# Loading q and k of the first five token pairs in other runs, with the heads paired anew

## The chip, the cores and the metric

The kernel runs on one core of a Trainium2 chip. The metric is the device time of one execution in microseconds; the time of a kernel is the median of several runs. The core's engines work side by side, each through its own list of instructions in order: TensorE (PE: matrix products; PEld is its loading of weights), VectorE (DVE), ScalarE (ACT), GpSimd (POOL), and SyncE (SP), which here mostly issues DMAs. They wait for each other through semaphores.

## The reference

Four sequences of 768 tokens, eight heads of 64. Three heads (0, 2, 6) attend causally to everything; the other five only to the first 4 tokens and to the last 64. The attention output, 3072 tokens by 512, goes through a gated feed-forward block with 1536 hidden columns.

```python
causal = rel >= 0
stream_keep = causal & (is_sink | ((rel >= 0) & (rel < window)))     # n_sink 4, window 64
mask = np.where(is_retrieval[head], causal, stream_keep)             # heads 0, 2, 6
a = softmax(np.where(mask, q @ k.T / 8, -1e9))
x = (a @ v)                      # (4, 8, 768, 64) -> (3072, 512)
g = x @ w_gate                   # (3072, 1536)
out = (g * sigmoid(g) * (x @ w_val)) @ w_out                         # (3072, 512), float32
```

All inputs are float32 in memory. The kernel computes in float16 with float32 sums.

## The kernel before, in words

The tokens are cut into 24 tiles of 128. Two tiles of one sequence make a pair; there are 12 pairs, in the order QP: (0, 0), (1, 0), (0, 1), (0, 2), (1, 1), (1, 2), and then sequences 2 and 3. A pair is what is loaded at a time: 256 tokens of q, of k or of v over all heads, 512 KB (`load`, L332; v is called x there). The weights come in 18 further loads of 512 KB. All loads are issued on SP, into a ring of 14 raw buffers; a load waits until the cast that reads its buffer's former content is done.

Each q or k load of the first five pairs (`XPE = 5`, L328) is two DMAs. One fills partitions 0 to 63 from heads 0 to 3, the other partitions 64 to 127 from heads 4 to 7; a partition gets four tokens of each of four heads, in runs of 1 KB (L338 to L344). From pair 5 on a load is one DMA over 128 partitions, in 512-byte runs of two tokens of each of eight heads (L345); v is always loaded so.

The loaded block is cast to float16 (`cast`, L402) so that a block of 128 columns holds two heads side by side. For the first five pairs TensorE transposes these blocks into PSUM (`transposes`, L442, product at L448), and ACT or DVE copies them into qT and kT, sorting the tokens out on the way (`evac`, L450). Later pairs are transposed by DMA (`dmat`, L435). The 128 rows of qT and kT are thus two heads of 64 rows. A score product (`scores`, L518, product at L533) uses 64 of the 128 rows, and the products of a unit alternate between the two halves. `PAIRS` (L165) says which heads share a block.

A tile's scores come in units of up to eight blocks of 128 by 128 (`plan`, L475). ACT takes the exponential of a unit at once (`exps`, L536). For the first four tiles (`LEAD = 4`) the mask is added into the scores by TensorE as products with an identity (`marks`, L495); later, DVE or POOL multiplies the exponentials with a mask of zeros and ones (`mask`, L547), which `FILLS` (L287) builds. The products with v (`values`, L557, product at L563) and a normalisation on DVE (`norm`, L566) follow, and the tile is transposed for the feed-forward products (`gate`, L721, product at L725; then ACT's tanh, two DVE steps, and `outproj`, product at L760). The keys and values of the 4 first tokens are copied into the first rows of later tiles (`sinks_k`, L462; `sinks_v`, L469).

Before all this TensorE runs ten products of the identity with itself, whose result is not used (`warm`, L309).

The order of the work is written out: every step is a task, and the string ORDER lists all tasks in one sequence from which each engine takes its own (L835). WAYS gives the engine of each task, SLOTS the buffer. A number of `FILL` (3700) or more in ORDER stands for a group of warming products; the kernel before has none.

Of the kernel before, what the change touches and what calls it, by code (L numbers as in the profile page):

```python
# [16 lines left out]
    "070004011K1L061I1J09031T1Q1R1S1o1p1w1x1U1V1y1W1X1f1g0A1q1r1z021d1k1e0C2K202223212B2C2Q2R2S292G2A"  # L17
    "081O1N1P1M1h1Y1Z1a1i1j0D2L2T0B1t1s1u2425261b1c1v2D2E2F2U2W2V2X2Z2a27282c2d1m1n2I2J052Y2b2h2l2m2n"
    "2r2s2o2w0h138r8s8t9192938w8x8y0n14948z90958p8u0E2O2P2N2M8m8n8o8q8v1l0g0z8c8d8e8h8i8j0y8S8T8U8X8Y"
    "0m118k8f8g8Z8l108a8V8W8b2p2q0i169697989B9C9D2e2f2i2g0G31393A3B0l1F9a9b9c9f9g2t2u2v2x0F30360o179E"  # L20
    "9F9h37383F3G3I3J0r1G9d9i9e9j3C3P3D3E3K3L0k1C9V9Q9W9X9R9S3b3c3T3H999A3U3V0J3j3r3s3t0H3234333M3N35"
    "3O3W3X3Y3Z3a0q1D9Y9Z0I3i3o9T9U3p3q3u3x3v3w3y3z0j199G9H9I9L9M9N2j3R3S2k2y2z3Q3d3e3f0p1A9O9J9P0Q55"
    "54523g3h45484E4F0x4041A9AAABAdAeAfA7ATAUACADAV0PAgAh494A2H530u0t15AOAP0w1E18AQARASAnAoAp0MA4A551"
    "580s9KA6A812AJAKAL0v1B0O1HAMAN0K3m3k3l3n0L4MAEAWAXAH0RAFAGAI0S5U590V669k9l9m9n4SAYAZAaAi4T0N4Q4R"
    "4P4N4U4V50579oAsAtAu56AvAw0Z5b4B4J4C4D42434644470cAjAk9p9q9r9s9t4G4H4K4I4LAlAmAxAyAz4Z4a4b4W4X4Y"
    "4e4f9u9v9w9x4j4p4q4u4v4c4d5T5a5Z0U4r9zA0A1A2A34m4s4O4g4t4h4n4i4k4l4oAqArAbAc0T5X5W5H5I5J5A5B5C5K"
    "B2B0B10d7o6E9y4w4x6o6l7E6n4y4z5L7G5M656C6BB3B4B5B7B8B9BABBBCBDBEBFBGBt5Q5d5j5k5e5f5g5h5iBvBwBx5Y"
    "C3BqBrBsBu0Y0bCACBCCBgBhBiBMBN0W686967ByBzBOC0C15N5O5R5P5cCDCEC2C40a7C6DBPBQBlBmBnC5C6C7BWBX5V5D"
    "5E5F5G5SBjBkBYBUBZBa6k6s6r5o5u5r5v5s5wBoBp0XC8C95l5m5p5n5q626L6M5x7I5yBbBcBdBeBf5t5z60636164BRBS"
    "BTBV7D7L7KCFCGCH7HBHBIBJBKBLCICJ6I6J6K6F6G6H6S6N6OCoCpCqCKCLCMCN0fDXDYDZCjCkClD8D9DaDbDADBDC6j6p"  # L30
    "6q7374756t6u70797JDNDODPDG0e7p7wCyCz6P71726Q6R6U6TCrCsD0D1D26Y6Z6a6d6eDQDRDDDEDFDH6v6V6W6X7SD6D3"
    "D4D5D7CeCfCgCPCQCRCSCT6m767T777A787B6w6x7r6yChCiCtCuCv6b6c7u7v7P7Q7R7MCOCwCxCmCnDSDTDU6A6f6g6h6i"
    "7N7OCUCVCWCXCZCaCYCbCc7F7U7V7WDVDW7X7g7h7a7b7c7t7d7e7f6zE4ELEJEMEOE1E2EGENEPEfEgE3E5EiEhEHEIEKEk"
    "ElEmDIDJDKEBECDLDMEDB6EpEqEjErCdDcDdDeDfDh7Y7i7j7m7kEnEo7l84857y7z81828B8380DiDjDkDmDnDo86877x8E"
    "8H8I8FDrDsDtDu7q7Z7n8K8M888N898A8C8D8LEd8GEVEWEXEQEREEEFESEYEZEsEt7s8O8J8P8QDwDxDyDzE6E7E8E9EAEa"
    "EbEcEeETEU8RFJFKFsFEFLFtFWG2FuFTFUFFDvDpFiDqDlE0FVFXFjFkFHFlFnFoFqDgFmFpFrEuFGFIFMFNGAG3G4G7G8G9"
    "GBFYFZFaFxFyFbFcFzG0G1FRG5G6FOFPFvFwFQFSFgEvEwExEyEzF0FdFeFfFhGCF1F2F4F5F6F9FAFBFCF3FDF7F8GDGEGF"
    "GGGHGIGJGKGLGMGNGOGRGPGSGTGQGWGUGVGXGY"
# [15 lines left out]
    "010523746A20796974080CAB6C17BD2493518B8DA51C93B8452163D10106040102241611232063220254440040006220"  # L54
    "616201436425612211161624043604454120646214300622320400616445611440622523226261404460004562163226"
    "112612440602263216203446045226106560612261304342246160122543246012162406140236445612242206143605"
    "0023111440102212311231000040220111550227010245020E1113A11049001182013501026303102104125F1004B212"
# [61 lines left out]
def kernel(  # L119
# [45 lines left out]
    PAIRS = [(0, 2), (4, 6), (1, 3), (5, 7)]  # L165
# [141 lines left out]
    warm_ps = []  # L307

    def warm(n=10):  # L309

        if not warm_ps:
            warm_ps.append(buf("o", [128, 512], FP, "warm"))
        for _ in range(n):
            nc.tensor.matmul(warm_ps[0], ident, ident.unsqueeze(1).to_broadcast([128, 4, 128]),
                             start=True, stop=True)
# [126 lines left out]
    def transposes(n, kd):  # L442

        tr = trs[n, kd] = buf("gv", [128, 8, 128], FH, "tr")
        for x in range(8):
            r, j = x // 4, x % 4
            to = x if kd == "q" else 4 * r + 2 * (j % 2) + j // 2
            nc.tensor.transpose(tr[:, to], hqs[n, kd][:, r, j], ident)  # L448
# [12 lines left out]

    def sinks_k(b, m):  # L462
# [3 lines left out]
        for cs, k, r in ((slice(0, 128), slice(0, 2), 1), (slice(0, 64), slice(1, 2), 0)):  # L466
# [28 lines left out]
    def marks(t, u):  # L495
# [339 lines left out]
    for number in P.order():  # L835
# [40 lines left out]
```

## Time and profile before

| | |
|---|---|
| median of three runs | 265.27 us (261.69 to 265.81) |
| the profiled execution | 262.36 us |
| its span, first to last instruction | 260.5 us |
| busy: TensorE, DVE, ACT, POOL | 243.2, 165.9, 139.2, 84.1 us |
| moved by DMA | 40.69 MB, 156 GB/s over the span |
| DMA packets | 68007 |
| q or k load of 256 KB, issue to landing (20 DMAs) | median 9.0 us (k), 8.6 us (q) |

The rows of the profile cut the span into 40 slices of 6.5 us; a digit is the busy share in tenths. A row of a timeline gives start, duration, engine, line, operation, the tiles written and read with their sizes, how many instructions are merged in the row, and in brackets the idle time before it and what ended it. A row of the windows gives the stretch and its length, the busy time and the number of instructions of PE, PEld, DVE, ACT and POOL, the granted TensorE clock, the mean share of time that the 16 DMA engines were busy (packets overlap, so it can pass 1), and GB/s. The 1.9 us between the span and the execution's time lie around the first and the last instruction.

### The profile page before, as it was taken

How to read it: one execution, taken by the hardware profiler on the slowest of the kernel's cores; microseconds unless marked ns; L12 is line 12 of the kernel's file. 1: busy time of each engine (PE TensorE's matmuls, PEld its weight loads, DVE VectorE, ACT ScalarE, POOL GpSimd, SP SyncE). 2: the span in 40 equal slices, each digit the busy share in tenths (PEclk: the TensorE clock that was granted, in tenths of full speed). 3: DMA queues.
4: the chain of work that ended last, by engine and by line, in shares of the span. 5: the costliest groups of instructions: out<-in, count | busy, mean ns of one | idle time of the engine just before them, and what ended most of it. 6: DMA issues, size and time to landing. Idle time of an engine off the chain costs nothing.

```text
span 260.5 us, 5165 instructions
## 1 busy us (share of the span) xinstructions
PE 243.2 (93%) x1998; PEld 127.9 (49%) x1998; DVE 165.9 (64%) x294; ACT 139.2 (53%) x219; POOL 84.1 (32%) x114
## 2 busy tenths in 40 slices
PE   6597987969999899989999999999999999999995
PEld 2365764446444445534464454555454554444443
DVE  2338897768497974609989678646773477883211
ACT  1568874738677476647585476644526713421120
POOL 7057945675432354183051018240014200000000
PEclk9999999979999999999999999999999999999999
DMA  6999999999699989999258841344010021101133
GB/s 152 230 236 325 285 219 264 226 273 332 155 327 276 236 168 220 300 254 255 45 77 177 193 102 20 83 116 128 1 23 20 20 64 52 69 3 40 40 126 115
DMA packets 68007, 40.69 MB, mean 156 GB/s; under 512 B 25360, under 2 KB 63504, under 8 KB 67984
## 3 DMA queue, kind: packets, MB, share of 16 engines
q1 hardware_dynamic: 66832, 38.35, 63.5%
q10 hardware_dynamic: 1152, 2.03, 2.1%
q8 instruction: 15, 0.25, 0.4%
q14 instruction: 8, 0.07, 0.1%
HBM read 28.31 MB, written 6.29 MB: 133 GB/s over the span
## 4 chain that ended last, share of the span: by engine, by line
PE 73%; DMA 13%; DVE 6%; SPq 3%; issue 2%; POOL 1%; ACT 1%; DVEq 0%; ACTq 0%
PE banks L725 40%; PE banks L760 22%; DMA raw<-in_v_dram 8%; PE banks L533 5%; PE banks L563 5%; SPq L340 3%; DMA kT<-hq 2%; DMA raw<-in_q_dram 2%; DVE e L553 2%; DVE sil L735 1%; DVE h L742 1%; POOL vt L206 1%; DVE xb L571 1%; PE banks L587 0%; POOL hq L206 0%
## 5 line engine op out<-in xcount | busy, mean ns | idle before, releaser
L545 ACT ACTIVATE e<-banks 128x1024 f16<-128x1024 f32 (+2 forms) x68 | 58.4, 908 | 31.0 <-PE banks L533 22.4
L725 PE MATMUL banks<-xt,wv_sb 128*128 128x512 f16 (+1 forms) x304 | 71.2, 371 | 2.8 <-POOL wv_sb L206 1.5
L725 PE MATMUL banks<-xt,wg_sb 128*128 128x512 f16 (+1 forms) x304 | 69.3, 368 | 1.6 <-POOL wg_sb L206 1.5
L731 ACT ACTIVATE sig<-banks 128x512 f32<-128x512 f32 (+1 forms) x76 | 43.1, 575 | 43.7 <-PE banks L725 38.5
L760 PE MATMUL banks<-wo_sb,h 128*128 128x512 f16 (+2 forms) x300 | 64.8, 371 | 0.0
L735 DVE SCALAR_TENSOR_TENSOR sil<-sig,banks 128x512 f32<-128x512 f32 (+1 forms) x76 | 49.3, 657 | 19.3 <-ACT sig L731 17.4
L742 DVE SCALAR_TENSOR_TENSOR h<-sil,banks 128x512 f16<-128x512 f32 (+1 forms) x76 | 49.0, 656 | 7.8 <-PE banks L725 5.0
L725 PEld LDWEIGHTS <-wg_sb 128*128 128x128 f16 x304 | 28.8, 97 | 33.1 <-POOL wg_sb L206 1.8
L725 PEld LDWEIGHTS <-wv_sb 128*128 128x128 f16 x304 | 28.3, 98 | 32.5 <-issue 2.8
L760 PEld LDWEIGHTS <-h 128*128 128x128 f16 x300 | 28.3, 98 | 32.4 <-issue 0.3
L553 POOL TENSOR_TENSOR e<-e,m 128x1024 f16<-128x1024 f16 (+1 forms) x12 | 22.6, 1883 | 32.4 <-ACT e L545 26.1
L553 DVE TENSOR_TENSOR e<-e,m 128x640 f16<-128x640 f16 (+1 forms) x26 | 20.3, 786 | 16.8 <-ACT e L545 16.6
L206 DVE COPY o_sb<-banks 128x512 f32<-128x512 f32 (+1 forms) x13 | 8.6, 660 | 25.0 <-PE banks L760 23.0
L206 POOL CAST vt<-raw 64x512 f16<-64x512 f32 x27 | 18.2, 675 | 17.7 <-DMA raw<-in_v_dram 14.3
L206 POOL CAST hq<-raw 128x1024 f16<-128x1024 f32 (+1 forms) x16 | 15.8, 989 | 24.7 <-DMA raw<-in_q_dram 11.9
L563 PE MATMUL banks<-vt,e 128*128 128x65 f16 x472 | 18.6, 195 | 4.0 <-POOL vt L206 3.1
L533 PE MATMUL banks<-qT,kT 64*128 64x128 f16 x472 | 21.0, 223 | 0.6 <-ACT e L545 0.4
L563 PEld LDWEIGHTS <-e 128*128 128x128 f16 x472 | 17.4, 98 | 8.4 <-issue 4.6
L204 ACT COPY o_sb<-banks 128x512 f32<-128x512 f32 (+1 forms) x12 | 6.9, 577 | 26.9 <-PE banks L760 23.1
L533 PEld LDWEIGHTS <-kT 64*128 64x128 f16 x472 | 15.1, 96 | 11.4 <-issue 10.0
L571 DVE TENSOR_TENSOR xb<-banks,rc 128x512 f16<-128x512 f32 x24 | 16.6, 691 | 0.8
L206 POOL COPY vt<-vt 2x330 f16<-2x330 f16 x12 | 5.8, 481 | 27.4 <-PE banks L563 27.1
(41 smaller groups left out, 117.2 us busy)
## 6 DMA issues: line engine op xcount, KB each, us to landing
raw<-in_v_dram SPq DMA_DIRECT2D x12, 512.0 KB, 7.5
out_dram<-o_sb SPq DMA_DIRECT2D x16, 256.0 KB, 2.3
raw<-in_k_dram SPq DMA_DIRECT2D x7, 512.0 KB, 5.9
raw<-in_q_dram SPq DMA_DIRECT2D x7, 512.0 KB, 5.8
raw<-in_moe_w_gate_dram SPq DMA_DIRECT2D x6, 512.0 KB, 9.8
raw<-in_moe_w_val_dram SPq DMA_DIRECT2D x6, 512.0 KB, 11.5
raw<-in_moe_w_out_dram SPq DMA_DIRECT2D x6, 512.0 KB, 8.0
raw<-in_k_dram SPq DMA_DIRECT2D x10, 256.0 KB, 9.0
```

Source lines behind the costliest of these rows:

```text
L206: ENG[task.way].tensor_copy(out=dst, in_=src)
L340: nc.sync.dma_start(out=r[64 * s_:64 * s_ + 64, :].rearrange("p (f x) -> p f x", f=4), in_={"q": q, "k": k}[kind][b, 4 * s_:4 * s_ + 4, sl ...
L533: nc.tensor.matmul(sc[:, c:c + n, :], weights, moving, start=first, stop=last)
L545: nc.scalar.activation(out=to, in_=src, func=AF.Exp, scale=scale)
L553: ENG[task().way].tensor_tensor(out=ev, in0=ev, in1=mm, op=ALU.mult)
L563: nc.tensor.matmul(avs[t][:, odd, n * 66:n * 66 + 65], ee, vv, start=(m == 0), stop=(m == len(bl) - 1))
L571: nc.vector.tensor_tensor(out=xb.rearrange("p n o d -> p o n d"), in0=av[:, :, :, 0:64], in1=rc.to_broadcast([128, 2, 4, 64]), op=ALU.mult)
L725: nc.tensor.matmul(ps, wsb[:, kk, j * 128:(j + 1) * 128], xt[:, kk, c[0]:c[1]], start=(kk == 0), stop=(kk == 3))
L731: nc.scalar.activation(out=sg[g, j, c], in_=gs[g, j, c], func=AF.Tanh, scale=0.5)
L735: nc.vector.scalar_tensor_tensor(out=sl[g, j, c], in0=sg.pop((g, j, c)), scalar=1.0, op0=ALU.add, in1=gs.pop((g, j, c)), op1=ALU.mult)
L742: nc.vector.scalar_tensor_tensor(out=hs[g, j][:, c[0]:c[1]], in0=sl.pop((g, j, c)), scalar=0.5, op0=ALU.mult, in1=vs.pop((g, j, c)), op1=A ...
L760: nc.tensor.matmul(o_open[g, tt, x], hs[g, j][:, tt * 128:(tt + 1) * 128], wo_sb[:, j, lo:hi], start=(j == 0), stop=(j == NJ - 1))
```

## The change

Pair 0 (`n < XOLD`, with `XOLD = 1`) loads q and k as pairs from 5 on do: one DMA over 128 partitions in 512-byte runs. Pairs 1 to 4 keep two DMAs of 256 KB for each load, but each fills one half of the columns of all 128 partitions: a partition gets eight tokens of one head out of four, in one run of 2 KB. Since a block of 128 columns now holds head h and head h + 4, `PAIRS` becomes (2, 6), (0, 4), (1, 5), (3, 7), and the cast, the copies out of PSUM, the places of the blocks in a unit, the marks, the mask fills and the indices into kT and qT follow. A group number in ORDER now also carries a PSUM bank, and four groups of warming products are added: 2 ahead of the transposes of k0, 4 ahead of those of q0, 5 ahead of those of q1, and 1 ahead of those of k1. ORDER and SLOTS are written anew; within each engine the tasks follow each other as before, apart from the four groups.

```diff
-    PAIRS = [(0, 2), (4, 6), (1, 3), (5, 7)]
+    PAIRS = [(2, 6), (0, 4), (1, 5), (3, 7)]
...
-    def warm(n=10):
-
-        if not warm_ps:
-            warm_ps.append(buf("o", [128, 512], FP, "warm"))
-        for _ in range(n):
-            nc.tensor.matmul(warm_ps[0], ident, ident.unsqueeze(1).to_broadcast([128, 4, 128]),
+    def warm(n=10, at=None):
+        if at is None:
+            to = buf("o", [128, 512], FP, "warm")
+        else:
+            to = banks[:, at * 512:at * 512 + 512]
+        for x in range(n):
+            nc.tensor.matmul(to, ident, ident.unsqueeze(1).to_broadcast([128, 4, 128]),
                              start=True, stop=True)
...
     XPE = 5
+    XOLD = 1
...
-            if kind != "x" and n < XPE:
+            if kind != "x" and XOLD <= n < XPE:
                 for s_ in range(2):
                     nc.sync.dma_start(
-                        out=r[64 * s_:64 * s_ + 64, :].rearrange("p (f x) -> p f x", f=4),
+                        out=r[:, 512 * s_:512 * s_ + 512],
                         in_={"q": q, "k": k}[kind][b, 4 * s_:4 * s_ + 4, sl, :].rearrange(
-                            "f (p j) d -> p f (j d)", j=4))
+                            "f (p j) d -> p f (j d)", j=8))
                 return
...
-        if n < XPE:
+        if XOLD <= n < XPE:
             js = slice(0, 8) if x is None else slice(4 * x, 4 * x + 4)
...
-        ks = slice(0, 2) if x is None else slice(x, x + 1)
+        fs = slice(0, 8) if x is None else slice(4 * x, 4 * x + 4)
         recast(T_c[n, kd, x],
-               hqs[n, kd][:, ks].rearrange("p k a (s d) -> p k s a d", s=2),
-               landed[kd, n].rearrange("p (k s r j d) -> p k s (r j) d", r=2, s=2, j=2, d=64)[:, ks])
+               hqs[n, kd].rearrange("p k a (s d) -> p s (k a) d", s=2)[:, :, fs],
+               landed[kd, n].rearrange("p (s f d) -> p s f d", s=2, d=64)[:, :, fs])
...
         dst = turned(n, kd)[:, m].rearrange("c k r x -> c (k r x)")
+        if n < XOLD:
+            tr = trs[n, kd].rearrange("c (f j) (m p) -> c m f j p", j=2, m=2)[:, m]
+            if kd == "q":
+                copy(T_ev[n, kd][m], dst.rearrange("c (f p j) -> c f p j", f=4, j=2),
+                     tr.rearrange("c f j p -> c f p j"))
+            else:
+                copy(T_ev[n, kd][m], dst.rearrange("c (f j p) -> c f j p", f=4, j=2), tr)
+            return
         if kd == "q":
-            copy(T_ev[n, kd][m],
-                 dst.rearrange("c (k r p j) -> c k r p j", k=2, r=2, j=4),
-                 trs[n, kd].rearrange("c (r j) (k m p) -> c m k r p j", r=2, k=2, m=2)[:, m])
+            copy(T_ev[n, kd][m], dst.rearrange("c (f n j) -> c f n j", f=4, j=8),
+                 trs[n, kd].rearrange("c j (m n f) -> c m f n j", m=2, f=4)[:, m])
             return
...
-        for cs, k, r in ((slice(0, 128), slice(0, 2), 1), (slice(0, 64), slice(1, 2), 0)):
+        for cs, k, r in ((slice(0, 128), slice(0, 2), 1), (slice(64, 128), slice(0, 1), 0)):
...
-            return [(0, BAND0, 3), (3, DIAG, 1), (4, BAND0, 2), (6, DIAG, 2)]
+            return [(0, BAND0, 2), (2, DIAG, 2), (4, BAND0, 3), (7, DIAG, 1)]
...
-        return kT[b % 2][:, kt, p % 2, p // 2]
+        return kT[b % 2][:, kt, PAIRS[p][0] // 2, PAIRS[p][0] % 2]
...
-        at = 1 if m is m2 else 0
+        at = 2 if m is m2 else 0
...
-            warm(number - P.FILL)
+            warm((number - P.FILL) % 16, (number - P.FILL) // 16)
```

More of the change, by code (lines that the diff above doesn't have):

```diff
@@ L16 @@
 ORDER = (
[L17 to L36, printed above, removed]
@@ L37 @@
-    "GBFYFZFaFxFyFbFcFzG0G1FRG5G6FOFPFvFwFQFSFgEvEwExEyEzF0FdFeFfFhGCF1F2F4F5F6F9FAFBFCF3FDF7F8GDGEGF"
-    "GGGHGIGJGKGLGMGNGOGRGPGSGTGQGWGUGVGXGY"
+    "00070306090A0C01041K1L08xy1T1I1Jy01Q1R1o1p0D1U1SyH1w1V1W0B1x1q0h1f1r1y1X0n02xh1z2K1g1d2021221k1e"
+    "1O2B1N0E232Q1P292C1M2R0g2L2S1h2A1Y1Z2G1i1a1t2T1s1u0m1v1j24251b2U2D262E2V2W0i1c2X2Z2F272h132a282c"
+    "0G1m2I1n2d142l2J2r2m052o0l8r2Y912s2b2O8w2n2w940F2P8s928z8t2N8p938x0z8u2M8y0o0y8m908c958n118h1l8o"
+    "0r8S108q8d8X8v8i8k168e8f8j0k8T8a8Y8U2p8V8g31968Z0J8l8W9B971F8b2q2e0H9C2f98392i9D309a0q2g3A9f9b3B"
@@ new lines @@
+    "172t9g9c2u0I362v9E1G372x0j3F3I3G9F9d1C9h3J0p9i3H383C9e3K3D9V0Q3j9j9Q3L3P3E329W0x343b9R9X3T33993c"
+    "9S1D3U3r0P9A3M3i3N3s3V3W0u3Z3t3X9Y19353a3o3O9T3Q0t3p3Y1A9Z3u3x3v9G0w9U3q3y9L3w0M9H2j3R3z2y9M3d9I"
+    "3e3S9N9O2k553f2z549J529P2H453g483h4E18404FA95141AdAA58A7ABAeATAf0sAC0vAU0O49AgAD0K15AO0LAVAhARAP"
+    "0R4A1EAn53AQA4Ao1B0SASAJA51HAp12AM9K59AKAEA6AWA83m0VALAH3kAN3n9kAF3l4M9lAXAG4S9mAIAY9n4TAiAZ4N5U"
+    "AsAa0N50Av4UAtAu4B424C4V6643Aw9p4JAj4D9q57469r449o4GAk9s4Q4H56Al4R4I4K4PAx0ZAm5b4ZAy4W4e4j9u4aAz"
@@ new lines @@
+    "5T479v4X4b4O9w0c4f4Y9t4p9x4u4L4q4c9z4v4rA05a4dA15Z4mA24s4g4h0U4tAq4i4kA34nAbAr4l4o5HAc5A5I5K0TB2"
+    "0d5BB06E5C4w4xB19yB36o7E6lB44y6nB75L5XB54z5WB8655JB96CBCBA6B7o5QBDBBBE7G5MBtBFBG5d5j5g5k0YBv5e0b"
+    "C30W5h5fBq5cBw5iCA5YBxBr0aBgCBBs6DBMBuBhCCByBiBNC0Bz5NBO5OCD5P6869BPC167CE5R5oBlC2C5C4Bm7CBWC65D"
+    "BQ5EBjBnBUC7BX5F5VBZ6kBk5G5u5r5vBYBoBa5S5sC85wBp625lC95m6s5t6L5p5x6MBb6r5n5yBeBc5z0X60Bd5qBR63Bf"
+    "CF61BS7IBHBTCGBVBI647DBJ6jCHCI7LBK7HBL6I6FCJ6N7K6JCoCK6G6K0fCL6p6O6HCp6SCMCq6qDXCNCj7JDYD8DZCk0e"
@@ new lines @@
+    "DaClD9DBDb73DA6t7470DCDN6u75DG79DOCy7pDP6P6QCz7wCr716RD1Cs6U72D06Y6d6ZDQD26eDD6a6TDR6V6vDE7SD66W"
+    "DFD3DH6X6mCeD4CPD5CfD7CQCgCR76CS776w6x787AChCT6yCt6A7T7B7rCi6bCu7P7M7u6cCwCv7QCm7vCO7RDSCx6fCnDT"
+    "6g7NCUDU6hCV7O6iCWCZCX7X7t7FCaCY6zCb7UCc7VB6DV7WCd7g7xDW7a7h7dE47bEL7e7cEJEM7fEOENE1EPEGE2EfE3E5"
+    "EiEgEHEkEhEIDIElEKEBDJEmDLDKECEp7ZDMDcEDEqEj7YDdEr7lDeDhDf7i7jEn7k7m84Eo7y7n8581Di8B7zDj8280Dm83"
+    "DnDkDo7q868E878HDr8IDs8F8JDt8KDu8M88898NEd8A8CEV8G8L8DEQEWEEEXER7sEYEFEsESEZ8O8PEtDw8QDzDx8RE6Dy"
@@ L39 @@
+    "E9DvE7EaE8EAETEbFJEcEeFsFKEUFEFtFLFWFuDpG2E0DqFTDgFiFUFFFHFVDlFXFlFjFnFkFmFqFoEuFpFrG3FMFGGAFIG7"
+    "FNG4FYG8FxG9FZGBFbFyFaG0FcFRFzG5G1FOG6FvFPFgFwFQEvFSEwEzExF0EyFdGCFeF1FfFhF4F2F5F3F6F9FAFBGDFCGE"
+    "FDF7GHGFF8GIGGGJGMGKGNGLGOGRGPGSGQGTGWGUGVGXGY"
 )
@@ L53 @@
 SLOTS = (
[L54 to L57, printed above, removed]
+    "010523746A20796974080CAB6C17B52493D18B8DA51C93B8452163D10106040102241611232063220254440040006220"
+    "616201436425612211161624043604454120646214300622320400616445611240622523226261404460404562163226"
+    "113612440602263216220446045226106560612261024342246160132543246012162406142236445612242206143605"
+    "0023111440102212311231000040220111550227010245020E1113A11049001182013501026302102104125F1004B212"
     "4I3021G3111D1000H0001M4112C1020K2010L2120J1121N0110024000104502081005A11046310472024E51010001511"
-    "1243311152025211109021000124000M1011K1000G1120J4105I5120H0121F4001D002280020C4000L2122B100112025"
-    "1149401142003241221502260123N5022541137510030103A111100004E521122000114M3002D2003C5012G4000H2110"
-    "L1015J2011K5121B2101I301080101F310012011"
+    "1243311152025211109021000124000M1011K1000G1120J4105I5120H0121F4001D302280020C4000L2122B300112025"
+    "1149401142003201221002260123N5022541137510033104A111101004E122012010115M3002D2004C1012G5000H1110"
+    "L4011J2014K5123B2103I301080104F300112001"
 )
@@ L162 @@
     scale = 1.0 / (D ** 0.5)
-    PAIRS = [(0, 2), (4, 6), (1, 3), (5, 7)]
+    PAIRS = [(2, 6), (0, 4), (1, 5), (3, 7)]
+    assert all(y == x + 4 for x, y in PAIRS)
     RINGS = {"raw": 14, "hq": 5, "e": 6, "xb": 3, "xt": 2, "sig": 2, "sil": 3,
@@ L285, in mask_fills @@
         return run
-    FILLS = [[(m0[:, 0:3], BAND0), (m0[:, 3:4], DIAG), (m0[:, 4:6], BAND0), (m0[:, 6:8], DIAG),
-              (m2[:, 2:5], DIAG), (m2[:, 1:2], OWN), (m1[:, 0:2], OWN)],
-             [(m2[:, 0:1], FAR), (m1[:, 2:4], FAR)]]
+    FILLS = [[(m0[:, 0:2], BAND0), (m0[:, 2:4], DIAG), (m0[:, 4:7], BAND0), (m0[:, 7:8], DIAG),
+              (m2[:, 0:3], DIAG), (m2[:, 3:4], OWN), (m1[:, 0:2], OWN)],
+             [(m2[:, 4:5], FAR), (m1[:, 2:4], FAR)]]
     kT = [const.tile([128, NT, 2, 2, 128], FH, name=f"kT{n}") for n in range(2)]
@@ L305, in fill1 @@
             nc.gpsimd.memset(vt[n][:, :, :, 64:66], 1.0)
-    warm_ps = []
-    def warm(n=10):
-        if not warm_ps:
-            warm_ps.append(buf("o", [128, 512], FP, "warm"))
-        for _ in range(n):
-            nc.tensor.matmul(warm_ps[0], ident, ident.unsqueeze(1).to_broadcast([128, 4, 128]),
+    def warm(n=10, at=None):
[5 more added lines that the diff above has]
+            nc.tensor.matmul(to, ident, ident.unsqueeze(1).to_broadcast([128, 4, 128]),
                              start=True, stop=True)
@@ L444, in transposes @@
         tr = trs[n, kd] = buf("gv", [128, 8, 128], FH, "tr")
[L445 to L448, printed above, removed]
+        for j in range(8):
+            nc.tensor.transpose(tr[:, j], hqs[n, kd][:, j // 4, j % 4], ident)
     def evac(n, kd, m):
         dst = turned(n, kd)[:, m].rearrange("c k r x -> c (k r x)")
+        if n < XOLD:
[6 more added lines that the diff above has]
+            return
         if kd == "q":
-            copy(T_ev[n, kd][m],
-                 dst.rearrange("c (k r p j) -> c k r p j", k=2, r=2, j=4),
-                 trs[n, kd].rearrange("c (r j) (k m p) -> c m k r p j", r=2, k=2, m=2)[:, m])
+            copy(T_ev[n, kd][m], dst.rearrange("c (f n j) -> c f n j", f=4, j=8),
+                 trs[n, kd].rearrange("c j (m n f) -> c m f n j", m=2, f=4)[:, m])
             return
         copy(T_ev[n, kd][m],
-             dst.rearrange("c (k l p i) -> c k l p i", k=2, l=4, i=2),
-             trs[n, kd].rearrange("c (l i) (k m p) -> c m k l p i", i=2, k=2, m=2)[:, m])
+             dst.rearrange(
+                 "c (f i n l) -> c f i n l", f=4, i=2, l=4),
+             trs[n, kd].rearrange("c (l i) (m n f) -> c m f i n l", i=2, m=2, f=4)[:, m])
     def sinks_k(b, m):
         T = kT[b % 2].rearrange("c t k r (j n) -> c t k r j n", j=2)
-        for cs, k, r in ((slice(0, 128), slice(0, 2), 1), (slice(0, 64), slice(1, 2), 0)):
+        for cs, k, r in ((slice(0, 128), slice(0, 2), 1), (slice(64, 128), slice(0, 1), 0)):
             recast(T_sk[b, m], T[cs, m, k, r, :, 0:NSINK // 2], T[cs, 0, k, r, :, 0:NSINK // 2])
@@ L482, in plan @@
                   ((2, i), (3, i), (2, -1), (3, -1))) for s_ in range(2)], 8, m1),
-              ([(0, 0, 0, 0), (0, 1, 5, i), (1, 0, 1, -1), (1, 1, 4, i),
-                (1, 0, 2, i), (1, 1, 6, 0), (0, 0, 3, i), (0, 1, 7, 0)], 8, m2)]
+              ([(0, 0, 0, 0), (0, 1, 4, i), (1, 0, 1, 0), (1, 1, 5, i),
+                (0, 0, 2, i), (1, 1, 6, -1), (1, 0, 3, i), (0, 1, 7, 0)], 8, m2)]
         kts = list(range(1, i))
@@ L488, in plan @@
             for x, kt in enumerate(ks):
-                unit += [(0, 0, 4 - len(ks) + x, kt), (0, 1, 4 + 2 * x, kt),
-                         (1, 1, 5 + 2 * x, kt)]
+                unit += [(0, 0, 4 - 2 * len(ks) + 2 * x, kt), (0, 1, 4 + x, kt),
+                         (1, 0, 5 - 2 * len(ks) + 2 * x, kt)]
             if unit:
-                us.append((unit, 4 + 2 * len(ks), None))
+                us.append((unit, 4 + len(ks), None))
         return us
@@ L499, in marks @@
         if TILES[t][1] == 0:
-            return [(0, BAND0, 3), (3, DIAG, 1), (4, BAND0, 2), (6, DIAG, 2)]
+            return [(0, BAND0, 2), (2, DIAG, 2), (4, BAND0, 3), (7, DIAG, 1)]
         if u == 0:
             return [(0, OWN, 2), (2, FAR, 2), (4, OWN, 2), (6, FAR, 2)]
-        return [(1, FAR, 1), (2, OWN, 1), (3, DIAG, 1), (4, DIAG, 2)]
+        return [(2, DIAG, 2), (4, DIAG, 1), (5, OWN, 1), (6, FAR, 1)]
     def block(t, p, kt):
@@ L525, in scores @@
             terms.append((c, 1, block(t, p, kt)[rows],
-                          qT[t // 2 % QB][rows, half, p % 2, p // 2].unsqueeze(1)))
+                          qT[t // 2 % QB][rows, half, PAIRS[p][0] // 2,
+                                          PAIRS[p][0] % 2].unsqueeze(1)))
         for c, n, weights, moving in terms:
```

## The prediction

> **What bounds the kernel now.** The profile's slice rows come first: who is busy, where.
>
> ```profile
> PE   6597987969999899989999999999999999999995
> ...
> DMA  6999999999699989999258841344010021101133
> ```
>
> TensorE is full from slice 11 (65 us) on; its holes lie in the first 60 us, where the DMA row is full. So I ask what TensorE waited for.
>
> ```profile
> PE banks L563 <- POOL vt L206: 3.1, 3, 2.3
> PE banks L448 <- ACT hq L204: 2.4, 2, 1.8
> PE banks L725 <- POOL wv_sb L206: 1.5, 2, 1.0
> PE banks L725 <- POOL wg_sb L206: 1.5, 1, 1.5
> ...
> PE banks L448 <- POOL hq L206: 1.3, 1, 1.3
> ```
>
> (Total us, times, longest.) Every one is a cast of something loaded: the engine named is the last link, the load is behind it. How fast do loads run? Windows of 5 us; the last two columns are the DMA share and GB/s, the third is DVE:
>
> ```profile
> 5.00:10.00 5.00, 2.56 (x17) 1.31 (x16) 1.35 (x6) 3.04 (x4) 1.09 (x5) 1.00 1.09 229
> 10.00:15.00 5.00, 3.68 (x34) 2.34 (x34) 2.58 (x4) 2.38 (x4) 2.04 (x5) 1.00 1.15 233
> ...
> 20.00:25.00 5.00, 3.92 (x85) 3.13 (x84) 3.90 (x12) 4.01 (x7) 3.61 (x6) 1.00 1.13 327
> 25.00:30.00 5.00, 4.64 (x65) 3.87 (x62) 4.57 (x10) 4.60 (x9) 4.67 (x7) 1.00 1.11 332
> ...
> 35.00:40.00 5.00, 3.53 (x42) 2.15 (x39) 4.77 (x11) 3.36 (x6) 2.09 (x2) 1.00 1.11 234
> ...
> 50.00:55.00 5.00, 2.68 (x45) 1.99 (x42) 4.04 (x6) 2.65 (x4) 3.59 (x5) 0.95 1.13 212
> 55.00:60.00 5.00, 5.00 (x57) 2.91 (x56) 2.88 (x5) 2.40 (x4) 3.44 (x6) 0.71 1.12 323
> 60.00:65.00 5.00, 5.00 (x59) 3.11 (x58) 4.59 (x9) 4.97 (x10) 2.42 (x4) 1.00 1.01 326
> ```
>
> The queue is equally full everywhere, but moves 212 to 239 GB/s while q and k of pairs 0 to 4 are in it (64-partition halves), and 323 to 332 where v and weights (all 128 partitions) or the 2 KB runs of w_out pass. The full-width loads of 512-byte runs are among the fast ones, so run length isn't it; width is. Last, the times that matter:
>
> ```profile
> 1.36 4.45 PE L314 MATMUL banks<-ident 128*128 128x512 f16 x10 [1.36 <-POOL ident L226]
> ...
> 9.38 1.03 PE L448 MATMUL banks<-ident,hq 128*128 128x128 f16 x8 [0.65 <-ACT hq L204]
> ...
> 15.28 1.04 PE L448 MATMUL banks<-ident,hq 128*128 128x128 f16 x8
> ...
> 18.97 0.62 PE L448 MATMUL banks<-ident,hq 128*128 128x128 f16 x8
> ...
> 27.42 1.48 PE L725 MATMUL banks<-xt,wg_sb 128*128 128x256 f16 x12
> ```
> ```profile
> 21.85 1.26 ACT L204 CAST vt<-raw 64x512 f16<-64x512 f32 x2 [0.43 <-DMA raw<-in_v_dram]
> ...
> 51.88 2.28 POOL L206 CAST vt<-raw 64x512 f16<-64x512 f32 x3 [1.10 <-DMA raw<-in_v_dram]
> ...
> 54.21 1.34 PE L563 MATMUL banks<-vt,e 128*128 128x65 f16 x25 [2.32 <-POOL vt L206]
> ```
>
> Eight transposes take 1.03 us until 16 us and 0.62 after: TensorE starts at a low clock, and the ten warming products don't change that. The first gate product runs at 27.42; v of pair 3 lands at 51.8 and holds TensorE for 2.32 us, after which the granted clock drops for one stretch (0.71 in 55 to 60).
>
> **Part by part.** The order of tasks on each engine is the same in both kernels, SP's included, but for four small warming groups on TensorE (2, 4, 5 and 1 products). So the replanning costs and gives nothing by itself; a few buffers of later stages have other numbers, which I take at zero (half a microsecond either way).
>
> *The loads.* 512 KB at 229 GB/s take 2.29 us; at 327 they take 1.60. Ten q and k loads gain 0.69 us each, 6.9 us. Their neighbours in the queue gain too: 25 us between 30 and 55 move 5.8 MB (220, 234, 257, 237, 212 GB/s in its windows), which at 327 take 17.7 us. Before 20 us it is 4.1 MB in 17.9 us, at 327 in 12.7. Together v of pair 3 can land some 12 us earlier, at about 40. [...] Pair 0 has two issues fewer, each about 0.6 us on SP, which brings all later issues 1.2 us forward.
>
> *The start.* k0 is 1.6 us of transfer in place of 2.3 and is cast about 0.7 us earlier (the cast waited until 5.64); q0, cast at 8.7, comes at 7.3; q1, at 11.0, comes at 8.9; k1, at 13.3, at 10.5. Warming: a product takes 0.445 us at the low clock, about 0.22 at full. The ten end at 5.8, two more at 6.7, transposes of k0 from 6.9, four products, transposes of q0, five products, transposes of q1, then the first scores. With the clock up by 8 us that is 6.9 + 1.0 + 0.9 + 0.6 + 1.1 + 0.6 = 11.1, against 12.56 now. With it low: 6.9 + 1.0 + 1.8 + 1.0 + 2.2 + 1.0 = 13.9, 1.3 us late, since the products stand ahead of transposes whose data is there. None of the four groups waits for anything; what stands behind them on TensorE is only those transposes and scores.
>
> [...] The row says that 4.45 us of products, then a gap of 1.8 us, left it low until about 17 us. [...] I take 11.1: the transition in the trace comes after 12.5 to 16.9 us, its first stretch without a gap.
>
> From there: score units of 1.0 us each at full clock, then six exponentials of 1.02 us (now ending at 21.4). They start at 12.0 in place of 14.2, and lose the pause of 1 us that the transposes of pair 1 made: they end at about 18.2. v of pair 1 (21.82 now) lands by 17.5, its ACT casts follow the exponentials: 3.4 us earlier than now, and so is the first gate product: 24.0.
>
> *27 to 58 us.* TensorE idles 0.46, 1.47, 0.50, 1.01 and 2.32 us here, 5.8 us in all, all for loads but the first, and a low clock costs half of one 3.4 us stretch, 1.7 us. With loads 12 us earlier none waits for a load. But something is late next: DVE. It is busy about 22 us between 27.1 and 54 (4.57, 4.43, 4.77, 3.24, 3.72 of each 5 in the windows, and the parts at both ends), where TensorE has 21.0. With a microsecond for imperfect meshing the stretch of 26.8 us can't go below 23: 3.8 to 4.5 us gained of 5.8, say 4.2. The clock: idle of half a microsecond at a time leaves it up (it stayed up after the 1.47), so 1.7.
>
> *After 58 us* TensorE has no wait above 0.84 us; it works off a fixed amount. Gain zero, between −0.5 and +1.5.
>
> *Shapes.* Casts move the same elements in runs of 64; zero (POOL's 1.04 us cast, ±5%, lies beside 30% idle). The evacuations read transposed columns with another stride. The nearest rows are 0.65 us apiece with a stride and 0.41 for the straight copy into xt: pairs 1 to 4 are taken at 0.65, pair 0 could fall by 0.2 each. Above: a fifth more on 16 copies is 2 us on DVE and ACT, mostly in the DVE-bound stretch. Mask fills, exponentials, masks and score products keep sizes and numbers; the pairs still alternate the two halves of the rows.
>
> Sum: 3.4 + 4.2 + 1.7 = 9.3 us. The profiled execution is 262.4 (260.5 span and 1.9 around it), giving 253.1. The median of the runs shown is 265.3, 2.9 above; part of that spread should be clock, which the change makes steadier. I say 253.5.
>
> **Rivals.**
> 1. *DVE keeps it all* (258). In 25 to 40 us DVE is 92% busy (4.57, 4.43 and 4.77 of each 5). If meshing costs as much as now, the stretch keeps its length: 3.4 us from the start and 1 of the clock stay. For it: the chain of waits runs through DVE from 23.7 to 35. Against: the 1.47 and 2.32 us waits end on casts that waited for DMA themselves.
> [...]
> 3. *Slower: the new runs are dealt out worse than the old* (269). Seven such loads precede v of pair 3. At 150 GB/s each takes 3.5 us, 1.2 more; 8.4 less 1.4 of pair 0, 7 us, all of it in the wait at 54.21, where every microsecond of v is one at the end. It decides from 2.49 us a load, 211 GB/s, down. For: no row has such a load. Against: its runs are longer than any in this stretch and go to all partitions.
>
> **Numbers.** Chances: 0.56 the forecast (own range 249.5 to 257), 0.18, 0.16 and 0.10 for the rivals. The range 249 to 262 leaves out the slower case and the tail below. A difference under 2% can't be told from none; the first rival lies at the edge (2.7% below the median, 1.7% below the profile): faster 0.66, within 2% 0.23, slower 0.11.
>
> **What would show it.** Right: 300 GB/s or more in 5 to 15 us; transposes of q1 in 0.62 us before 12; first gate product near 24; no wait above 1 us ahead of the values that need v of pair 3; DVE at 90% from 24 to 45. [...]

## The result, and the profile after

| | before | after |
|---|---|---|
| median | 263.48 us (4 runs, 261.57 to 265.81) | 250.43 us (4 runs, 249.54 to 250.69) |
| profiled execution, its span | 262.36, 260.5 us | 250.21, 248.3 us |
| TensorE busy | 243.2 us (93%) | 240.2 us (97%) |

The ratio of the times is 0.952, 95% interval 0.944 to 0.960. The forecast was 253.5 us, 3.1 too many. Medians are of all executions, while a ratio leaves out the few that were over 1.5% slower than the fastest of their kernel and, for the experiments, is taken against executions of the kernel before on the same chip (medians 261.92 to 264.31 us).

The slice rows of the kernel after: TensorE is full from the second slice on, but for one 8 and the last slice, and the DMA row falls off in its 19th slice, at 112 us, where it did so in its 20th, at 124 us (a slice is a fortieth of the span).

```profile
PE   7999999999999999899999999999999999999995
...
DMA  6999999958999999992598312460110223001142
```

The longest waits of TensorE (total us, times, longest). No wait for a cast of q, k or a weight is left, and one of 0.5 us for a cast of v, where the five rows of before made 9.8 us:

```profile
PE banks L314 <- POOL ident L227: 1.4, 1, 1.4
PE banks L734 <- issue: 0.7, 1, 0.7
PE banks L734 <- DMA xt<-xb: 0.6, 1, 0.6
PE banks L734 <- DVE sil L744: 0.5, 1, 0.5
PE banks L542 <- ACT e L554: 0.5, 1, 0.5
PE banks L572 <- ACT vt L205: 0.5, 1, 0.5
...
```

Windows of the kernel after; columns as before, the last two are the DMA share and GB/s, the third is DVE:

```profile
5.00:10.00 5.00, 5.00 (x41) 2.97 (x39) 2.80 (x8) 3.23 (x6) 2.25 (x7) 1.00 1.08 363
10.00:15.00 5.00, 5.00 (x78) 3.50 (x77) 2.42 (x5) 4.12 (x6) 4.11 (x9) 1.00 1.14 323
...
30.00:35.00 5.00, 5.00 (x64) 3.11 (x63) 4.92 (x11) 4.00 (x8) 3.49 (x4) 1.00 1.10 353
35.00:40.00 5.00, 5.00 (x57) 2.64 (x54) 4.80 (x10) 3.22 (x5) 3.02 (x3) 1.00 1.11 345
40.00:45.00 5.00, 5.00 (x74) 3.19 (x73) 4.81 (x10) 4.54 (x8) 4.85 (x6) 1.00 1.12 335
45.00:50.00 5.00, 5.00 (x63) 3.06 (x61) 4.93 (x10) 4.38 (x8) 3.26 (x5) 1.00 1.10 351
50.00:55.00 5.00, 5.00 (x60) 2.91 (x57) 2.84 (x7) 4.18 (x10) 4.06 (x6) 1.00 0.67 207
```

The stretch that ran at 229 GB/s runs at 363; between 5 and 50 us no window is below 323, and from 50 us the share of the DMA engines falls to 0.67. From 30 to 50 us TensorE is full and DVE 97% busy at the same time. Rows of TensorE's timeline, to be set beside those at 1.36, 9.38, 27.42 and 54.21 of before:

```profile
1.36 5.13 PE L314 MATMUL banks<-ident 128*128 128x512 f16 x12 [1.36 <-POOL ident L227]
6.33 0.61 PE L448 MATMUL banks<-ident,hq 128*128 128x128 f16 x8
6.78 1.03 PE L314 MATMUL banks<-ident 128*128 128x512 f16 x4
7.64 0.61 PE L448 MATMUL banks<-ident,hq 128*128 128x128 f16 x8
8.09 1.24 PE L314 MATMUL banks<-ident 128*128 128x512 f16 x5
9.17 0.61 PE L448 MATMUL banks<-ident,hq 128*128 128x128 f16 x8
```
```profile
22.12 1.48 PE L734 MATMUL banks<-xt,wg_sb 128*128 128x256 f16 x12
...
43.00 0.92 PE L572 MATMUL banks<-vt,e 128*128 128x65 f16 x25
```

The transposes take 0.61 us from the first on: the clock is up by 6.3 us. At the start the clock must be read from such durations. The column of the granted clock shows 1.00 in 5 to 15 us of before, where eight transposes take 1.03 us. TensorE does the same work in the same order in both kernels, so the same product can be looked up in both traces. What it is ahead tells where the time went:

| the same product | before | after | ahead |
|---|---|---|---|
| second product of the first scores' marks | 12.88 | 9.72 | 3.2 us |
| first gate product | 27.42 | 22.12 | 5.3 |
| first value product behind v of pair 3 | 54.21 | 43.00 | 11.2 |
| a score product behind the clock's low stretch | 59.77 | 47.02 | 12.7 |
| late output product | 256.48 | 244.26 | 12.2 |

So 5.3 us came from the start, 7.4 from the stretch up to 60 us, and 0.5 was lost after it.

### The profile page after: what moved, and what is told of

It reads as the page before. It is cut to its first block, busy times and chain, and to the rows that moved or that the text cites. A ratio compares the mean times of both kernels' runs of the same rounds, so it can differ in the third digit from the quotient of the medians.

```text
span 248.3 us, 5187 instructions
## 1 busy us (share of the span) xinstructions
PE 240.2 (97%) x2010; PEld 126.3 (51%) x2010; DVE 165.7 (67%) x294; ACT 140.1 (56%) x219; POOL 84.7 (34%) x114
## 4 chain that ended last, share of the span: by engine, by line
PE 76%; DMA 8%; SPq 7%; DVE 4%; ACT 2%; issue 2%; POOL 0%; DVEq 0%; POOLq 0%; ACTq 0%
PE banks L734 43%; PE banks L769 18%; PE banks L542 6%; PE banks L572 4%; SPq L438 3%; PE banks L314 3%; DMA kT<-hq 2%; DMA raw<-in_q_dram 2%; SPq L347 2%; ACT e L554 2%; DMA xt<-xb 2%; DMA out_dram<-o_sb 2%; PE banks L448 1%; DVE e L562 1%; SPq L590 1%
## 5 line engine op out<-in xcount | busy, mean ns | idle before, releaser
L542 PE MATMUL banks<-qT,kT 64*128 64x128 f16 x472 | 20.2, 217 | 1.1 <-ACT e L554 0.5
L542 PEld LDWEIGHTS <-kT 64*128 64x128 f16 x472 | 14.6, 94 | 11.3 <-issue 8.9
L572 PEld LDWEIGHTS <-e 128*128 128x128 f16 x472 | 16.7, 97 | 5.0 <-ACT vt L205 0.8
```

The lines of the kernel that those rows point to most:

```text
L542: nc.tensor.matmul(sc[:, c:c + n, :], weights, moving, start=first, stop=last)
L572: nc.tensor.matmul(avs[t][:, odd, n * 66:n * 66 + 65], ee, vv, start=(m == 0), stop=(m == len(bl) - 1))
```

## The experiments

Names in a_ start from the changed kernel, names in b_ from the kernel before. The changed kernel itself, run again (a_again, below), came out at 0.960 [0.948, 0.972] for 0.952. So ratios between 0.952 and 0.963 don't tell its variants apart. What can be told apart are places in the traces up to 60 us: there two profiles of the changed kernel agree within 0.1 us, while at the end they are 2.2 us apart.

### Is it the number of partitions, or the length of the runs?

```diff
-    XOLD = 1
+    XOLD = 5
```

> The changed kernel with pairs 1 to 4 loaded like pair 0: one DMA over 128 partitions, 512-byte runs. Theory (the number of partitions sets the rate, not the length of the run): q and k go at about 305 GB/s, as v does, 0.25 us a load more than in 2 KB runs, 2 us by v of pair 3, which has slack: 250 to 251.5 us, no slow stretch near 230 GB/s before 50 us. Rival (the 2 KB runs made it fast): the rate falls back towards 230 GB/s and the time to 258 or more.

Measured: 252.56 us (252.20 to 253.16), 0.963 of before [0.958, 0.969]. Its windows:

```profile
5.00:10.00 5.00, 5.00 (x37) 2.71 (x36) 2.60 (x7) 2.96 (x6) 1.68 (x6) 1.00 1.20 290
10.00:15.00 5.00, 5.00 (x78) 3.43 (x76) 2.04 (x4) 4.09 (x7) 3.11 (x7) 1.00 1.20 290
...
30.00:35.00 5.00, 5.00 (x57) 3.78 (x56) 4.72 (x12) 3.73 (x8) 3.40 (x5) 1.00 1.12 332
```

Runs half as long as the 1 KB of before, and still 290 GB/s for 229: most of the gain stays without long runs. The score product of the table above comes at 49.60, which is 10.2 us ahead of before in place of 12.7. The 2 KB runs add a part (290 to 363), and against the expectation that part has little slack to hide in: v of pair 1 comes later (cast by POOL at 19.26 for 16.26), and the first gate product stands at 24.36, 2.2 us later than in the changed kernel.

The other way round: take a load that is fast, leave its runs and sources, and cut it by partitions.

```diff
+            if kind == "x" and n < XPE:
+                for s_ in range(2):
+                    half = slice(pi * 256 + 128 * s_, pi * 256 + 128 * s_ + 128)
+                    nc.sync.dma_start(
+                        out=r[64 * s_:64 * s_ + 64, :].rearrange("p (h x) -> p h x", h=H),
+                        in_=v[b, :, half, :].rearrange("h (p j) d -> p h (j d)", j=2))
+                return
```

> The changed kernel with v of the first five pairs split in two DMAs, one for partitions 0 to 63 and one for 64 to 127; runs of 512 bytes and their sources as they were. Theory (64 partitions at a time is what is slow): while v0 passes (10 to 12 us) the rate falls from about 310 to 230 GB/s or less, v of pair 1 lands 1 us or more later, first gate product 23 or later. Rival (q and k were slow for their sources or runs): 300 GB/s or more as before, nothing moves by more than 0.5 us.

Measured (two executions): 255.53 us (255.22 and 255.83), 0.973 of before [0.957, 0.989]. The windows in which v0 passes (10 to 12 us) and in which v1 does (14 to 16), first of the changed kernel, then of this one:

```profile
10.00:12.00 2.00, 2.00 (x33) 1.40 (x32) 1.10 (x2) 1.41 (x2) 1.87 (x5) 1.00 1.17 313
14.00:16.00 2.00, 2.00 (x37) 1.51 (x37) 1.03 (x2) 2.00 (x4) 1.94 (x3) 1.00 1.17 319
```
```profile
10.00:12.00 2.00, 2.00 (x33) 1.40 (x27) 0.97 (x3) 1.73 (x2) 1.74 (x5) 1.00 1.20 247
14.00:16.00 2.00, 1.55 (x26) 1.12 (x23) 1.34 (x3) 2.00 (x3) 1.90 (x4) 1.00 1.23 236
```

Two halves of 64 partitions turn a 313 GB/s load into a 247 GB/s one. That is near the rate that q and k had before (229 to 239). It isn't the second DMA that does it, since q and k of the changed kernel are two DMAs too, and run at 363. POOL's casts of v0 and of v of pair 1 begin 0.7 us later, where 1 us or more was expected. The first gate product does not move (22.07; the expectation had 23 or later), though the scores began 0.3 us earlier in this execution. What follows moves: 1.4 us are lost by 28 us, in a wait for a weight's cast, and the rest later.

Both halves under way together, in the layout of before (the five numbers are the tasks that load k0, q0, q1, k1 and q2):

```diff
+                    eng = nc.scalar if s_ and (kind, n) in FIRST_LOADS else nc.sync
-                    nc.sync.dma_start(
+                    eng.dma_start(
...
+    FIRST_LOADS = [("k", 0), ("q", 0), ("q", 1), ("k", 1), ("q", 2)]
...
-    for number in P.order():
+    ahead = [7, 6, 9, 10, 12]
+    for number in ahead + [x for x in P.order() if x not in ahead]:
```

> The kernel before with its own 64-partition loads, but of the first five (k0, q0, q1, k1, q2) the half for partitions 64 to 127 is issued on ACT's queue, so that both halves are under way at once. [...] Rival (the source pattern or the 1 KB runs in four heads are slow): 229 GB/s as before.

Measured: 262.92 us (260.81 to 265.44), 1.002 of before [0.998, 1.005]; 260 GB/s in 5 to 10 us and 264 in 10 to 15. The cast of q2 begins at 14.06 for 15.93 and the first gate product is at 25.58, 1.8 us earlier, but the whole is no faster. The rate is above the 229 and 233 of before, so the rival is missed. Finer windows show two rates, not one in between:

```profile
6.00:7.00 1.00, 0.00 (x0) 0.00 (x0) 0.00 (x0) 0.99 (x2) 0.23 (x2) 1.00 1.14 235
7.00:8.00 1.00, 0.53 (x7) 0.36 (x8) 0.00 (x0) 0.81 (x2) 0.00 (x0) 1.00 1.13 235
...
9.00:10.00 1.00, 0.58 (x8) 0.31 (x6) 0.38 (x1) 0.00 (x0) 0.00 (x0) 0.62 1.10 333
10.00:11.00 1.00, 0.08 (x1) 0.08 (x2) 0.91 (x2) 0.82 (x2) 0.61 (x1) 0.50 1.13 300
```

From 4 to 8 us it is as slow as before, although both halves of k0, q0, q1 and k1 are issued by 3.7 us; then it reaches 300 and more. In the kernel before, too, the first loads pass at 305 GB/s in 3 to 4 us, and those in the next microsecond at 224. So 64 partitions at a time were not slow at every moment, and this run is no proof of what makes them slow. Over windows of 2 to 5 us, 229 to 247 GB/s were measured for such loads (before and a_vhalves). That loads in halves of 64 partitions are slower is shown by the two runs above (229 against 290, 247 against 313); why, no run shows.

### The start: ACT's table, and one DMA or two

The profile after holds a surprise. ACT's rows, before and after:

```profile
5.64 1.28 ACT L204 ACT_TABLE_LOAD   x1 [5.64 <-DMA raw<-in_k_dram]
6.93 1.14 ACT L204 CAST hq<-raw 128x512 f16<-128x512 f32 x2
```
```profile
0.73 1.28 ACT L205 ACT_TABLE_LOAD   x1 [0.73 <-PEq L866]
4.89 1.14 ACT L205 CAST hq<-raw 128x512 f16<-128x512 f32 x2 [2.87 <-DMA raw<-in_k_dram]
```

In the kernel before, the first cast needs two DMAs, and the instruction ahead of it, the loading of the function table, already waits for k0. With one DMA for k0 only the cast waits. That the number of DMAs decides it is tested by the next run.

```diff
-    XOLD = 1
+    XOLD = 0
```

> The changed kernel with pair 0 in two DMAs of 2 KB runs as pairs 1 to 4. Theory: the transfer of k0 is no slower, but the first cast on ACT then waits for two DMAs, and that wait stands ahead of the loading of ACT's function table, so the table (1.28 us) is loaded after k0 lands: first cast at 6 us or later in place of 4.9, first gate product about 1 us later, 251 to 252 us. Rival (one or two DMAs for k0 is all one, only bytes count): table loaded at 0.7, first gate product at 22 or earlier, 250 us.

Measured: 252.06 us (250.44 to 253.68), 0.961 of before [0.954, 0.968]. The table is loaded at 4.59, the first cast is at 5.88, the first gate product at 23.29, 1.2 us later than in the changed kernel, as expected. The next run gives the same loads an early table:

```diff
+    early = const.tile([128, 2], FH, name="early")
+    nc.gpsimd.memset(early[:, 0:1], 0.0)
+    nc.scalar.copy(out=early[:, 1:2], in_=early[:, 0:1])
```

> The changed kernel with pair 0 in 2 KB runs as pairs 1 to 4, and the one-column copy on ACT that has the function table loaded at once. Theory (a_all2k lost its 1.2 us by the late table alone): table at 0.7, first cast by 4.7 to 4.9, first gate product at 21.5 to 22.1, 249.5 to 250.5 us. Rival (two DMAs for k0 are late by themselves): first gate product at 23, 251.5 us.

Measured: 251.83 us (251.50 to 252.09), 0.960 of before [0.955, 0.965]. The first cast is at 4.56 now, but q0, which has two DMAs too, is cast at 7.54 and not at 6.67, and the first gate product is at 22.76. So of the 1.2 us about half is the table, and half is that two DMAs for each of k0 and q0 are late by themselves: SP issues six DMAs of 0.6 us by 4.6 us for k0, q0 and q1, in place of four by 3.8, and DMA is busy only 0.88 in 5 to 10 us.

The table by itself, the same three lines in the kernel before:

> The kernel before with one copy of a single column on ACT ahead of everything, so that ACT's function table (1.28 us) is loaded at once and not after k0 lands. Theory (the table's place is a part of the gain at the start, but the loads bound what follows): first cast at 5.7 in place of 6.9, the first transposes 1.2 us earlier, first gate product within 0.5 us of 27.4 since v of pair 1 sets it, 262 to 263 us in the profile. Rival (the table is worth its 1.28 us by itself): first gate product 1.2 us earlier and the end too.

Measured: 264.34 us (262.35 to 266.17), 1.007 of before [1.003, 1.011]. The first cast is at 5.83, the first transposes 1.1 us earlier, the first gate product 0.6 earlier (26.84), and by 40 us all of it is gone: TensorE waits for the same loads. The table alone made nothing faster, and the profiled execution (265.43 us) lies above the 262 to 263 expected. In it the clock also rose by 5 us, was low again until 15 us (granted clock 0.50 in the second row, third column from the end), and once more after 55 us (0.60 in 55 to 60):

```profile
5.00:10.00 5.00, 2.18 (x18) 1.22 (x16) 1.36 (x7) 1.76 (x3) 1.09 (x5) 0.82 1.14 217
10.00:15.00 5.00, 3.56 (x33) 2.29 (x34) 2.58 (x4) 2.62 (x4) 2.03 (x5) 0.50 1.16 213
```

### The warming products

```diff
         else:
-            warm((number - P.FILL) % 16, (number - P.FILL) // 16)
+            continue
```

> The changed kernel without the four groups of warming products (the ten first ones stay). Theory (the products lift the clock early): transposes and scores take 1.03 and 0.61 us until 12 to 15 us, first gate product 1 to 2.5 us later, end 251.5 to 253 us. Rival (they are in the way, the loads do it all): first gate product at 22 or earlier, end 250 us or less.

Measured: 250.08 us (248.07 to 250.52), 0.952 of before [0.945, 0.958], the same ratio as the changed kernel's; the first gate product is at 21.65. The theory was wrong. The repetition, beside the changed kernel:

> Again the changed kernel without the four warming groups, now beside the changed kernel itself on one chip. [...] Rival (the groups are worth more than 1 us): more than 1 us slower.

> The changed kernel itself, for the comparison with the run without warming groups on the same chip: 250 to 251 us.

Measured on one chip: 249.10 us without the groups (248.04 to 249.46), 0.948 of before [0.938, 0.958]; 252.11 us with them (251.57 to 253.01), 0.960 [0.948, 0.972]. The changed kernel missed its expectation by 1.1 us, and the rival, over 1 us slower without the groups, failed: it was 3.0 us faster. TensorE's rows without the groups:

```profile
1.36 3.96 PE L314 MATMUL banks<-ident 128*128 128x512 f16 x10 [1.36 <-POOL ident L227]
5.60 0.92 PE L448 MATMUL banks<-ident,hq 128*128 128x128 f16 x8 [0.27 <-ACT hq L205]
7.35 0.62 PE L448 MATMUL banks<-ident,hq 128*128 128x128 f16 x8 [0.84 <-ACT hq L205]
8.84 0.62 PE L448 MATMUL banks<-ident,hq 128*128 128x128 f16 x8 [0.87 <-POOL hq L207]
```

The transposes of q1 are at full clock at 8.84; the ten first products had lifted it by 4.7 us, and it stayed up over gaps of 0.8 to 0.9 us (in b_table, with gaps of 1.2 to 1.5 us, it fell: granted clock 0.50 in 10 to 15 us). With the groups the same transposes start at 9.17, behind products. The groups cost 0.5 to 0.6 us at the first gate product and 0.7 to 0.9 by 43 us. The rest of the difference of 3 us arises after 75 us, where two profiles of the changed kernel itself also come to differ by 2.2 us, and is not settled. The kernel without the groups is the fastest of all that ran: its four times here lie below the four with groups, though by 1.2% only, and the two intervals against before overlap.

The groups alone, in the kernel before (same four places, banks and numbers):

```diff
+            extra = {"trk0": (2, 1), "trq0": (4, 1), "trq1": (5, 2), "trk1": (1, 0)}
+            if P.tasks[number].name in extra:
+                warm(*extra[P.tasks[number].name])
             running.append(P.tasks[number])
```

> The kernel before with the four groups of warming products alone, at the same places. Theory (loads bound the start): the clock rises before 12 us, but v of pair 1 still lands near 21.8 and the first gate product stays within 1 us of 27.4: 261.5 to 263.5 us. Rival (warming is a part of the gain by itself): first gate product at 25, 259 to 260 us.

Measured: 263.71 us (260.27 to 265.53), 1.002 of before [0.997, 1.007]. In the profile the first gate product comes at 25.81, 1.6 us earlier (the theory had at most 1), but by 60 us only 0.5 us of it is left: TensorE stands 3.0 us in all before its value products, for casts of v. Warming won nothing while the loads were late, and in the two runs above it wasn't needed when they were early.

### Does DVE bound the stretch to 50 us?

The changed kernel with four useless steps of DVE, behind the normalisation of tiles 4 to 7:

```diff
+    idle = const.tile([128, 2, 512], FP, name="idle")
+    nc.vector.memset(idle, 0.0)
...
             P.tasks[number].run()
+            if P.tasks[number].name in ("nm4", "nm5", "nm6", "nm7"):
+                nc.vector.tensor_reduce(out=idle[:, 1], in_=idle[:, 0].unsqueeze(2),
+                                        axis=mybir.AxisListType.X, op=ALU.max)
```

> The changed kernel with four useless DVE steps of 0.69 us each (reductions of a scratch tile), one behind the normalisation of each of the tiles 4 to 7, all between 30 and 50 us. Theory of the prediction (DVE bounds that stretch): what follows is 2 us or more later, end 252.5 to 253. Rival (DVE is full there but what it holds has slack against TensorE): under 0.7 us, 250 to 251.

Measured: 253.12 us (252.24 to 256.96), 0.963 of before [0.954, 0.971]. The products at 57 us are 2.5 us later than in the changed kernel. Of these, 0.5 stand already at 10 us, before the first added step, where the clock rose later in this execution (the transposes of k0 still take 0.98 us). So 2.0 us remain for 2.8 us of added DVE work. The added steps run at 34.4, 37.0, 48.3 and 54.1 us, the last outside the stretch that was meant. DVE's backlog now reaches past 50 us:

```profile
45.00:50.00 5.00, 4.84 (x65) 2.76 (x62) 4.90 (x9) 3.74 (x6) 3.85 (x5) 1.00 1.10 351
50.00:55.00 5.00, 4.82 (x66) 3.13 (x67) 4.97 (x10) 4.28 (x9) 1.92 (x4) 1.00 0.64 200
```

DVE is at 4.97 of 5 in 50 to 55 us, where the changed kernel has 2.84. So DVE has little slack in this stretch, and yet in the changed kernel it hardly holds TensorE up: one wait of 0.5 us for it, at 25.42, stands between 22 and 60 us. It just fits.

## Why the prediction was right or wrong

**What bounds the kernel** was right: the loads. The rate of q and k hung on the 64 partitions; a_all512 (290 GB/s for 229) and a_vhalves (247 for 313) show it from both sides. The 327 GB/s of the sum, the row of 20 to 25 us of before, were an estimate for the new loads and low, since with the 2 KB runs 363 were measured in 5 to 10 us. After 20 us that makes no difference, because TensorE then waits for no load; v of pair 3 is cast at 40.35, where "at about 40" was forecast. Why halves of 64 partitions are slow stays open.

**The start**: 3.4 us forecast, 5.3 measured. One step that failed is "k0 is cast about 0.7 us earlier": the cast went from 6.93 to 4.89, 2.0 us, since the function table no longer waits for k0. The row of the table's loading stood in the profile of before, its idle time ended by the k0 load, and was not counted. Going back to two DMAs costs 1.2 us at the first gate product, and about half of that is the table, as a_2k_table and a_all2k together show. The other casts were early too: q0 at 6.67 where 7.3 was forecast, q1 at 8.05 for 8.9, k1 at 9.45 for 10.5.

With this the scores began at 9.62 in place of 11.1. It is not a load that sets the 9.62: TensorE has no idle time between 1.36 and 15 us and works off its products one behind another. In the terms of the forecast's sum, the transposes of k0 start at 6.33 for 6.9 (0.6 us), they hold TensorE for 0.45 us at full clock where 1.0 at the low one was counted (0.55), and those of q0 and q1 hold it for 0.45 each where 0.6 was counted (0.3). The early casts are what allowed it: transposes of q1 at 9.17 need a cast before the forecast's. The last 0.4 us of the miss lie between the scores and the gate product, 12.5 us for 12.9.

**The clock.** The forecast took its 11.1, the clock up by 8 us, against the row of before, where 4.45 us of products had left it low; that the groups would lift it was the author's estimate. It was up at 6.3. But the sum had put this to the groups' account, and that no run shows. Without the groups the ten products were enough in both profiles (by 4.7 us in a_nowarm2), as in b_table, where the clock rose by 5 us and fell again in the gaps. With them, in five of the seven profiles of the changed kernel and its variants, the tenth product still ran at the low clock (0.43 us from start to start, 0.22 later), and the clock rose at about 6 to 7 us, during the groups or the transposes of k0. Whether it would have risen there without them no run shows. So that the transposes came out at 0.61 us was forecast, but that the kernel needs the groups for it was not borne out. When the clock rises differs from one profile to the next, with the ten products starting at 1.36 us in each: by 4.7 us in a_nowarm2, not before 16.9 in before. What decides it no run shows. The groups stand in the way by 0.5 to 0.9 us, as the forecast's worse case had feared, though by less than its 1.3.

**27 to 58 us**: 4.2 + 1.7 forecast, 7.4 measured: all of the 5.8 us of waits and the 1.7 of the clock (granted before: 0.74, 0.50, 0.50 and 0.55 in the microseconds from 54 to 58; after: 1.00) came back. The step "the stretch can't go below 23" failed: it took 20.9 (22.12 to 43.00). The 22 us of DVE work in it were counted right (22.55 in 27.42 to 54.21), and a_dve shows that DVE is near its limit. But it was taken as if all of that work had to be done when TensorE passes the value products. It doesn't. In the kernel before, these three steps of DVE are over, or nearly so, when the value product starts at 54.21; in the kernel after they come behind the one at 43.00:

```profile
52.21 0.82 DVE L553 TENSOR_TENSOR e<-e,m 128x1024 f16<-128x1024 f16 x1
52.95 0.68 DVE L206 COPY kT<-banks 128x512 f16<-128x512 f16 x1
53.66 0.68 DVE L210 TENSOR_REDUCE vt<-raw 64x512 f16<-64x512 f32 x1
```
```profile
43.48 0.80 DVE L562 TENSOR_TENSOR e<-e,m 128x1024 f16<-128x1024 f16 x1
44.20 0.68 DVE L207 COPY kT<-banks 128x512 f16<-128x512 f16 x1
44.91 0.68 DVE L211 TENSOR_REDUCE vt<-raw 64x512 f16<-64x512 f32 x1
```

That is 2.2 us of work put off, about the 2.1 by which the stretch is shorter than 23. DVE works it off at 4.81 and 4.93 of 5 until 50 us, and TensorE meanwhile has products that don't need it.

**After 58 us**: zero forecast, between −0.5 and +1.5; −0.5 measured. **Shapes**: DVE's busy time is 165.7 us for 165.9, ACT's 140.1 for 139.2; taking them at zero was right in the main.

**The sum**: 253.1 for the profiled execution, 250.2 measured; the miss of 2.9 us is 1.9 at the start and 1.5 in the stretch after it, while the 0.5 lost at the end takes a little back. That the times would grow steadier came true: 249.54 to 250.69 us, where before had 261.57 to 265.81. Of the rivals, the first (DVE keeps it all) had a true premise and a wrong consequence; the third is ruled out by 363 GB/s, and so is a rate that stays near 230.

## What to carry to other kernels

Look at the rate of a full DMA queue by stretches: where it drops while the queue stays busy, look for loads that fill only 64 partitions, and try them over all 128; here that paid even at half the run length (290 GB/s in 512-byte runs for 229 in 1 KB runs). When an engine is counted as the bound of a stretch, ask which of its work must be finished at the end of the stretch; what may lag behind doesn't lengthen it (2.2 us of DVE work here). Once a new kernel is fast, test its parts one at a time: the warming products here cost 0.5 to 0.9 us up to 43 us in the kernel that the loads had already cured.

## What the runs showed that was not expected

- ACT loaded its function table (1.28 us) ahead of its first cast. Where that cast needed two DMAs (before, a_all2k), the table waited for data and was loaded at 5.64 and 4.59 us; with one DMA, or with an early copy on ACT, at 0.73.
- Splitting a 512-byte-run load into two halves of 64 partitions took it from 313 to 247 GB/s; two halves of a 1 KB-run load on two queues got 260 to 264 over 5 us, 226 to 235 at first and 300 to 333 later.
- By the durations of the products, the clock rose within the ten warming products in some executions (by 4.7 us in a_nowarm2, 4.8 in b_table) and not before 16.9 us in the profile of before.
- Two profiles of one and the same kernel, 0.1 us apart at 60 us, were 2.2 us apart at the end.
